# A conformer block on one core: the query projection in seven products instead of eight, placed at the turn of chunks

## The chip, the cores and the metric

The kernel runs on one core of one Trainium2 chip. The core has five engines that run beside each other: TensorE (PE in the profile) multiplies matrices into PSUM, VectorE (DVE) and ScalarE (ACT) do the elementwise work and empty PSUM, GpSimd (POOL) does small things, and SyncE (SP) issues the DMAs. The metric is the device time of one execution in microseconds (us), lower is better.

## The reference, cut to what matters

The reference is one conformer block on an input of 2 batches of 4000 tokens with 512 features: a feed-forward layer, self-attention with one head, a convolution module, a second feed-forward layer, each with a layer norm and a residual. What the change touches is the attention's query side:

```
h = _layernorm(x1)
q, k, v = h @ w_q, h @ w_k, h @ w_v
scores = einsum('btd,bsd->bts', q, k) * scale
attn = einsum('bts,bsd->btd', softmax(scores), v) @ w_o
x2 = x1 + attn
h = _layernorm(x2) @ w_pw1        # the first convolution product, 512 -> 1024
h = h[..., :512] * sigmoid(h[..., 512:])
```

## The kernel before, in words

**Tiling.** The tokens are cut into 16 chunks (`NCK`), 8 in each batch. A chunk has 512 tokens, the last of each batch 416, since 8 x 512 is more than 4000. The kernel has three stages: first feed-forward (to some 405 us), attention with the convolution beside it (to some 1380 us), and second feed-forward. The weights of queries and keys are folded into one matrix `M` beforehand, so that queries are `h M` and keys are `h` itself; likewise `w_v` and `w_o`.

**The attention loop.** `attention` (L2070) runs over the chunks `g` and, in each, over 32 steps `kt`, one for each tile of 128 keys. Two steps are called a pair, four make a quad. In chunk 0 each step makes a plain score product. From chunk 1 on steps 0, 1 and 30 are plain, step 31 holds the 32 keys that are left of the last tile, and steps 2 to 29 are seven *score quads* (`score_quad`, L2013). A quad multiplies 2x2 blocks with seven block products instead of eight (the Strassen-Winograd form): VectorE makes sums of the operands beforehand, TensorE computes products 5, 1, 6, 2, 7, 3, 4 in that order, and sums of products are joined on the way. A product here is four matmuls of 256 columns (208 in the chunks of 416 tokens). A quad has three PSUM banks, numbered 0, 1 and 2: `c`, `x` and `h`. Product 5 goes to `x` and ScalarE copies it to an SBUF tile m5; product 1 goes to `c`, and ScalarE copies that to `h`; product 6 is accumulated on `h`, and VectorE adds `h` and m5 into `x`; product 2 is accumulated on `c`; product 7 on `h`, and VectorE adds `h` and m5 once more; product 3 is accumulated on `x`, product 4 on `h`. So each product on `h` waits for an ACT or DVE instruction on it, and the next quad's banks are those of this one.

**The values** (`pv`, L1850) are in the same form: for each pair seven products of two matmuls, accumulated over the pairs in other banks. Products 2 and 4 of all pairs are put off to steps 2 to 6 of the next chunk (`late_third`, `units_late`, L2165). The exponentials of a pair therefore stay in a ring of `NR` places from when they are written to the next chunk's step 6 at most. At steps 0 and 1 the last sums of the chunk before are joined, and its row of softmax denominators (`lrow`) is written, stored to HBM and read back by query (`sum_row`, `sums_by_query`).

**The queries.** For a chunk `c`, `fetch_queries` (L1702) loads the tokens, transposed by DMA, to one of two slots of `lnT`; `q_group` (L1686) then makes 128 of the 512 query features with four matmuls of 512 columns, and ScalarE copies them out. Four groups make a chunk's queries: 16 matmuls of 512 columns (or 416) and four copies, at steps 16, 17 and 20 of the chunk before (for chunk 2 at steps 3 and 5). `q_sums` at steps 27 to 30 forms the sums of the queries that the score quads want.

**The convolution** of chunk `t` runs beside the attention of chunk `t + 2`: two *conv quads* at steps 2 to 7 on banks 7, 5, 3 and 4, and ScalarE's `taps_beside` at steps 8, 11, 14 and 17. Chunk 7 (416 tokens, its last tile shared with the other batch) is done plainly: `pair` (L2851) makes one of four feature blocks, two at steps 24 and 28 of chunk 8, two at steps 3 and 5 of chunk 9, and calls the taps of chunk 6 itself.

**What sets the order.** The program isn't emitted as written. `Plan` (L112) records every instruction, estimates its duration, and lists them anew engine by engine with a look-ahead of 16 us (8 us for TensorE), in six passes; each engine then runs its list strictly in order. `S.front(1000)` gives score quads a preference. All instructions are therefore recorded at one line, L95, and groups in the profile are told apart by tile names. In those names `s` are PSUM banks 0 to 3 and `y` banks 4 to 7. `work` holds `lnT`, `M`, the queries and the values' form 4; `xt` the sums for score quads and two of the value forms; `keys` keys and values; `sums` the exponentials; `wff` the convolution's work space. A row names what is written, then what is read: `s<-work` with 512 columns is a query group, `s<-xt` and `s<-work,keys` with 256 columns are score products, `y<-sums,keys` is a value product.

```
L2013  def score_quad(self, g, q, step):            # steps 0 to 3 = four kt
L2070  def attention(self, old, hook, between):
L2068      ASIDE = {3: (5, 7), 4: (5, 7), 5: (5, 7), 6: (5, 7), 16: (0,), 20: (0,)}   # banks lent to other products
L2753          S.planned(16000, 8000)
```

## Time and profile before

| | us |
|---|---|
| median of 3 runs (lowest to highest) | 1858.07 (1857.97 to 1860.41) |
| the profiled execution's own time | 1860.54 |
| its span, first to last instruction | 1855.0 |
| PE busy in the span | 1838.5 (99%) |
| DVE busy | 1439.8 (78%) |
| ACT busy | 1355.7 (73%) |
| POOL busy | 140.8 (8%) |
| mean granted TensorE clock | 0.999 of full speed |

The profiled execution took 1860.54 us, 2.47 us above the median of the three runs and close to the slowest of them; 5.54 us of it lie outside the span. PE's busy time counts matmuls that overlap in the pipeline, so it shows where PE had something under way, not that it did as much as it can. What one matmul costs is read from the timeline, from the start of one group to the start of the next.

### The profile page before, as it was taken

To read this page: it belongs to the slowest core of one execution; us is meant where nothing else is said; L and a number is where in the kernel's file an instruction comes from. 1 tells how busy PE (TensorE), PEld (TensorE's weight loads), DVE (VectorE), ACT (ScalarE), POOL (GpSimd) and SP (SyncE) were. 2 spreads that over 40 slices of the span, in tenths; PEclk is the share of its full clock that TensorE was granted. 3 is DMA by queue.
4 is the path that set the end of the run, shared out by engine and by line. 5 is a ranking of instruction groups with operands and counts; after the bars stand their busy time and mean duration, and the time that the engine had idled before them with its cause. 6 is when DMAs were issued, how large, how long until landed. Compare 5 with 4: busy or idle time off the path is not lost.

```text
span 1855.0 us, 40175 instructions
## 1 busy us (share of the span) xinstructions
PE 1838.5 (99%) x15922; PEld 1497.3 (81%) x15922; DVE 1439.8 (78%) x3108; ACT 1355.7 (73%) x2402; POOL 140.8 (8%) x356
## 2 busy tenths in 40 slices
PE   9999999999999999999999999999999999999998
PEld 6888888866878787888777788788875888888887
DVE  8889898868566777667875666766778988888896
ACT  6887777754656777677776876777768778778776
POOL 3000000000000000000000000000011000000000
PEclk9999999999999999999999999999999999999999
DMA  8333344288545655457954434543475222221211
GB/s 201 85 90 85 82 113 99 69 246 238 161 135 141 171 163 157 116 146 169 246 133 132 120 110 118 141 119 111 114 224 164 62 69 72 66 58 48 57 39 57
DMA packets 312521, 228.50 MB, mean 123 GB/s; under 512 B 191154, under 2 KB 283125, under 8 KB 312068
## 3 DMA queue, kind: packets, MB, share of 16 engines
q1 hardware_dynamic: 311796, 225.59, 45.2%
q8 instruction: 127, 2.08, 0.5%
q14 instruction: 70, 0.57, 0.1%
q10 hardware_dynamic: 528, 0.26, 0.0%
HBM read 128.99 MB, written 55.82 MB: 100 GB/s over the span
## 4 chain that ended last, share of the span: by engine, by line
PE 96%; ACT 1%; DVE 1%; DMA 1%; SPq 1%; issue 0%; POOL 0%; DVEq 0%
PE y L95 50%; PE s L95 45%; DVE work L95 1%; SPq L95 1%; ACT work L95 1%; DMA wff<-in_w_ff_a_dram 0%; DMA xt<-v12d 0%; DVE wff L95 0%; DMA keys<-tailsd 0%; ACT keys L95 0%; ACT sums L95 0%; DVE xt L95 0%; DMA work<-lrowd 0%; ACT xt L95 0%; DVE s L95 0%
## 5 line engine op out<-in xcount | busy, mean ns | idle before, releaser
L95 ACT ACTIVATE sums<-s 128x512 bf16<-128x512 f32 (+4 forms) x498 | 291.0, 585 | 131.2 <-PE s L95 127.4
L95 DVE TENSOR_TENSOR sums<-sums 128x512 bf16<-128x512 bf16 (+3 forms) x528 | 202.0, 399 | 87.2 <-ACT sums L95 75.4
L95 ACT ACTIVATE keys<-s 128x512 bf16<-128x512 f32 (+3 forms) x275 | 156.9, 574 | 134.4 <-PE s L95 110.9
L95 PE MATMUL y<-work,keys 128*128 128x256 bf16 x1920 | 244.5, 273 | 0.0
L95 PE MATMUL s<-sums 128*128 128x256 bf16 (+1 forms) x1428 | 212.5, 272 | 0.3 <-DVE s L95 0.3
L95 ACT ACTIVATE work<-xt,work 128x512 bf16<-128x512 bf16 x268 | 205.2, 785 | 8.8 <-DVE work L95 5.6
L95 PE MATMUL y<-wff,keys 128*128 128x256 bf16 (+3 forms) x1592 | 209.3, 276 | 0.0
L95 PEld LDWEIGHTS y<-work,keys 128*128 128x128 bf16 x1920 | 187.6, 98 | 22.6 <-DVE work L95 0.2
L95 PE MATMUL s<-work,keys 128*128 128x256 bf16 (+5 forms) x1400 | 205.3, 284 | 0.1
L95 PE MATMUL y<-sums,keys 128*128 128x256 bf16 (+1 forms) x1440 | 204.1, 270 | 0.1
L95 PE MATMUL y<-work,wff 128*128 128x256 bf16 (+3 forms) x1308 | 195.2, 272 | 0.8 <-ACT keys L95 0.8
L95 DVE TENSOR_TENSOR keys<-keys 128x1024 bf16<-128x1024 bf16 (+2 forms) x262 | 170.4, 664 | 22.6 <-ACT keys L95 17.8
L95 PEld LDWEIGHTS y<-wff,keys 128*128 128x128 bf16 (+1 forms) x1592 | 151.2, 98 | 29.9 <-issue 3.3
L95 DVE BATCH_NORM_STATS2 work<-xt 128x6 f32<-128x512 bf16 x251 | 163.0, 681 | 2.5 <-DMA xt<-in_x_dram 1.8
L95 PEld LDWEIGHTS y<-sums,keys 128*128 128x128 bf16 x1440 | 138.0, 98 | 25.3 <-issue 3.3
L95 PEld LDWEIGHTS s<-sums 128*128 128x128 bf16 x1428 | 139.0, 98 | 22.7 <-DVE s L95 0.6
L95 POOL TENSOR_TENSOR work<-work 128x4 f32<-128x4 f32 (+3 forms) x107 | 91.6, 859 | 765.1 <-DVE work L95 752.6
L95 PE MATMUL y<-sums,xt 128*128 128x256 bf16 (+1 forms) x960 | 146.1, 270 | 0.8 <-DMA xt<-v12d 0.8
L95 DVE TENSOR_TENSOR s<-s,xt 128x512 f32<-128x512 f32 (+1 forms) x105 | 72.4, 690 | 95.2 <-PE s L95 65.3
L95 PEld LDWEIGHTS s<-work,keys 128*128 128x128 bf16 (+1 forms) x1400 | 112.9, 97 | 40.9 <-ACT sums L95 2.2
L95 PEld LDWEIGHTS y<-work,wff 128*128 128x128 bf16 x1308 | 126.2, 98 | 17.9 <-issue 1.5
L95 PE MATMUL s<-xt,keys 128*128 128x256 bf16 (+1 forms) x872 | 132.5, 270 | 1.9 <-DVE s L95 1.7
(155 smaller groups left out, 3286.3 us busy)
## 6 DMA issues: line engine op xcount, KB each, us to landing
xt<-kfd SPq DMA_DIRECT2D x98, 384.0 KB, 3.3
xt<-v12d SPq DMA_DIRECT2D x105, 256.0 KB, 3.1
xd<-xt SPq DMA_DIRECT2D x28, 512.0 KB, 3.1
xt<-xd SPq DMA_DIRECT2D x28, 512.0 KB, 4.8
out_dram<-xt SPq DMA_DIRECT2D x14, 512.0 KB, 2.9
xt<-in_x_dram SPq DMA_DIRECT2D x13, 512.0 KB, 4.3
dcvd<-wff SPq DMA_DIRECT2D x48, 128.0 KB, 4.2
keys<-dcvd SPq DMA_DIRECT2D x12, 512.0 KB, 4.0
```

What stands on the lines that cost most here:

```text
L95: return getattr(eng, self.name)(*self.args, **self.kw)
```

## The change

The queries of chunks 2 to 15 are made by a new quad, `query_quad`, with 28 matmuls of 256 (or 208) columns in place of 16 of 512 (or 416). Chunks 0 and 1 keep `q_group`. The quad has the same banks 0, 1, 2 and the same order of products as a score quad. For chunk `g + 2` its first part (products 5 and 1) stands at step 31 of chunk `g`, the others (6 and 2; 7 and 3; 4) at steps 0 and 1 of chunk `g + 1`, around the plain scores of these steps; those now go to banks 0 and 1, before to 0 and 2. ScalarE makes five copies for it and VectorE two sums from PSUM.

It wants sums of the weights, made once (`query_weights`, four DVE instructions in steps 21 to 24 of chunk 0, the last one in place in `M`), and sums of the tokens (`query_sums`, four DVE instructions for each chunk, in steps 23 to 26 of the chunk two ahead of it). The tokens are thus fetched two chunks ahead, at step 9, into slot 1 of `lnT` (chunk 2's at step 21 of chunk 0, and into slot 1, before slot 0).

For room, the ring of exponentials has 18 places, before 20; the row of denominators moves to the convolution's work space, and the token sums stand there too. Since a place is now written again sooner, product 4 of the late values is dealt out differently over steps 3 to 6. The whole first convolution product of chunk 7 now stands in chunk 9, at steps 2 to 5, with three banks lent in turn, and the taps of chunk 6 at the steps of every other chunk.

```diff
-        self.NR, self.NTS = 20, 6
+        self.NR, self.NTS = 18, 6
...
+        oMF, o = o, o + 2 * row
...
-        lrow, self.b_lrow = C.view(oACC + 2048, CHUNK, F32, parts=1), C.buf("lrow", oACC + 2048, 4 * CHUNK)
-        self.lrow, self.lflat = lrow.rearrange("o (p t) -> o t p", t=TPC), lrow
...
+        homes = ((C, oACC + 2048), (C, oACC + 3072), (E, oMF))
+        self.MF = [R.view(o, D).rearrange("p (j f) -> p j f", j=2) for R, o in homes]
+        self.b_MF = [R.buf("MF", o, 2 * D) for R, o in homes]
...
+        lrow, self.b_lrow = W.view(12288, CHUNK, F32, parts=1), W.buf("lrow", 12288, 4 * CHUNK)
+        self.lrow, self.lflat = lrow.rearrange("o (p t) -> o t p", t=TPC), lrow
+        self.TF = [W.view(8192 + n * 1024, 2 * HC).rearrange("p (j k) -> p j k", j=2) for n in range(3)]
+        self.b_TF = [W.buf("TF", 8192 + n * 1024, 4 * HC) for n in range(3)]
...
-        return 1 if b or qc == 1 or qc > 2 else 0
+        return 1 if b or qc else 0
...
     def next_queries(self, g, kt, at):
-        if g + 1 < NCK and g != 1 and at <= kt < at + TPC:
-            self.fetch_queries((g + 1) // TCB, (g + 1) % TCB, kt - at)
-        if g == 0 and 24 <= kt < 24 + TPC:
-            self.fetch_queries(0, 2, kt - 24)
-        if self.any_score:
-            plan = {3: (0,), 4: (1,), 14: (2,), 16: (3,)} if g == 1 else {14: (0,), 16: (1,), 18: (2,), 20: (3,)}
-        else:
-            plan = {3: (0, 1), 5: (2, 3)} if g == 1 else {16: (0,), 17: (1, 2), 20: (3,)}
-        if g + 1 < NCK:
+        ahead = 1 if self.any_score or g == 0 else 2
+        if g + ahead < NCK and at <= kt < at + TPC:
+            self.fetch_queries((g + ahead) // TCB, (g + ahead) % TCB, kt - at)
+        if g == 0 and kt == 21 and not self.any_score:
+            self.fetch_queries(0, 2, 0)
+        if g + 1 < NCK and (g == 0 or self.any_score):
+            plan = {14: (0,), 16: (1,), 18: (2,), 20: (3,)} if self.any_score else {16: (0,), 17: (1, 2), 20: (3,)}
             for dc in plan.get(kt, ()):
                 self.q_group((g + 1) // TCB, (g + 1) % TCB, dc)
+
+    def query_weights(self, step):
+
+        a11, a12, a21, a22 = [self.M[:, 2 * k:2 * k + 2, f * HD:(f + 1) * HD] for f in range(2) for k in range(2)]
+        s1, s2, s4 = self.MF
+        b1, b2, b4 = [[b] for b in self.b_MF]
+        out, x, y, op, rd, wr = ((s1, a21, a22, ALU.add, [], b1), (s2, s1, a11, ALU.subtract, b1, b2),
+                                 (s4, a12, s2, ALU.subtract, b2, b4), (a21, a11, a21, ALU.subtract, [], [self.b_M]))[step]
+        self.S.op("DVE", lambda e: e.tensor_tensor(out=out, in0=x, in1=y, op=op), reads=rd + [self.b_M], writes=wr)
+
+    def query_sums(self, g, step):
+
+        b, qc = divmod(g, TCB)
+        sl, hw = self.query_slot(b, qc), width(g) // 2
+        lin = self.queries(qc, sl)[0]
+        at = lambda k, h: lin[:, 2 * k:2 * k + 2, h * hw:(h + 1) * hw]
+        t1, t2, t4 = [x[:, :, 0:hw] for x in self.TF]
+        b1, b2, b4 = [[x] for x in self.b_TF]
+        out, x, y, rd, wr = ((t1, at(0, 1), at(0, 0), [], b1), (t2, at(1, 1), t1, b1, b2), (t4, at(1, 0), t2, b2, b4),
+                             (at(0, 1), at(1, 1), at(0, 1), [], self.b_lnT[sl]))[step]
+        self.S.op("DVE", lambda e: e.tensor_tensor(out=out, in0=x, in1=y, op=ALU.subtract),
+                  reads=rd + self.b_lnT[sl], writes=wr)
+
+    def query_quad(self, g, step):
+
+        b, qc = divmod(g, TCB)
+        S, s, sl, W, hw = self.S, qc % 2, self.query_slot(b, qc), width(g), width(g) // 2
+        (c, b_c), (x, b_x), (h, b_h) = [self.bank(k) for k in range(3)]
+        m5, b_m5 = self.m5s[:, 0:W], self.b_m5s
+        lin = self.queries(qc, sl)[0]
+        two = lambda ap: ap.rearrange("p (u k) -> p u k", u=2)
+        part = lambda f, k: (lambda u, j: self.M[:, 2 * k + j, f * HD + u * 128:f * HD + (u + 1) * 128], self.b_M)
+        form = lambda m: (lambda u, j: self.MF[m][:, j, u * 128:(u + 1) * 128], self.b_MF[m])
+        at = lambda k, q: (lambda j: lin[:, 2 * k + j, q * hw:(q + 1) * hw], self.b_lnT[sl])
+        t_form = lambda m: (lambda j: self.TF[m][:, j, 0:hw], [self.b_TF[m]])
+        forms = {1: (part(0, 0), at(0, 0)), 2: (part(0, 1), at(1, 0)), 3: (form(2), at(1, 1)), 4: (part(1, 1), t_form(2)),
+                 5: (form(0), t_form(0)), 6: (form(1), t_form(1)), 7: (part(1, 0), at(0, 1))}
+        home = lambda f, q: (self.qT[s][:, 2 * f:2 * f + 2, q * hw:(q + 1) * hw], self.b_qT[s][2 * f:2 * f + 2])
+
+        def product(k, ps, b_ps, start=False):
+            (a, b_a), (m, b_m) = forms[k]
+            for u in range(2):
+                for j in range(2):
+                    self.mm(ps[:, u * hw:(u + 1) * hw], a(u, j), m(j), start and u == 0 and j == 0, u == 1 and j == 1,
+                            [b_a, *b_m], b_ps, skip_group_check=True)
+
+        def copy(src, b_src, f, q):
+            out, b_out = home(f, q)
+            self.act(out, two(src[:, 0:W]), AF.Copy, [b_src], b_out)
+
+        if step == 0:
+            product(5, x, b_x, True)
+            self.act(m5, x[:, 0:W], AF.Copy, [b_x], [b_m5])
+            product(1, c, b_c, True)
+            self.act(h[:, 0:W], c[:, 0:W], AF.Copy, [b_c], [b_h])
+        elif step == 1:
+            product(6, h, b_h)
+            S.op("DVE", lambda e: e.tensor_tensor(out=x[:, 0:W], in0=h[:, 0:W], in1=m5, op=ALU.add), reads=[b_h, b_m5], writes=[b_x])
+            product(2, c, b_c)
+            copy(c, b_c, 0, 0)
+        elif step == 2:
+            product(7, h, b_h)
+            out, b_out = home(1, 1)
+            S.op("DVE", lambda e: e.tensor_tensor(out=out, in0=two(h[:, 0:W]), in1=two(m5), op=ALU.add), reads=[b_h, b_m5], writes=b_out)
+            product(3, x, b_x)
+            copy(x, b_x, 0, 1)
+        else:
+            product(4, h, b_h)
+            copy(h, b_h, 1, 0)
     def p_home(self, g, i):
...
             product(4, h, b_h)
             exp(h[:, 0:W], b_h, 21)
-    ASIDE = {3: (5, 7), 4: (5, 7), 5: (5, 7), 6: (5, 7), 16: (0,), 20: (0,)}
+    ASIDE = {2: (5, 7, 3), 3: (3, 5, 7), 4: (7, 3, 5), 5: (5, 7, 3), 6: (3, 5, 7), 16: (0,), 20: (0,)}
     def attention(self, old, hook, between):
...
                     self.ring = [0, 1, 2]
                 else:
                     self.ring, self.rings["S"] = list(self.ASIDE.get(kt, (0, 1))), 0
+                if 0 < g < NCK - 1 and kt < 2:
+                    self.query_quad(g + 1, 1 if kt == 0 else 3)
                 if plain and kt < KT - 1 or kt < 2 or kt == KT - 2:
-                    ps, b_ps = self.scores(g, kt, None if plain else self.bank((0, 2)[kt] if kt < 2 else 0))
+                    ps, b_ps = self.scores(g, kt, None if plain else self.bank(kt if kt < 2 else 0))
                     if kt < KT - 2:
                         self.exp_pair(g, kt, ps, b_ps)
                     else:
...
                     S.front(1000)
                     self.score_quad(g, *divmod(kt - 2, 4))
                     S.front(0)
+                if g < NCK - 2:
+                    if kt == KT - 1:
+                        self.query_quad(g + 2, 0)
+                    if 23 <= kt < 27:
+                        self.query_sums(g + 2, kt - 23)
+                if 0 < g < NCK - 1 and kt == 0:
+                    self.query_quad(g + 1, 2)
+                if g == 0 and 21 <= kt < 25:
+                    self.query_weights(kt - 21)
                 if g == 0 and kt < 2:
                     self.pop(old // 2 if kt == 0 else old - old // 2)
                 if kt == (21 if g == 0 else 24 if g < NCK - 1 else 16):
...
         elif kt < 7:
             m = (kt - 2) * 6
             self.late_third(o, 2, range(m, min(m + 6, PAIRS)))
-            self.late_third(o, 4, range(max(m - PAIRS, 0), max(m + 6 - PAIRS, 0)))
+            self.late_third(o, 4, {3: range(1), 4: range(1, 3), 5: range(3, 9), 6: range(9, PAIRS)}.get(kt, ()))
         if kt == 9:
             self.ln_conv = self.nxt("ln", self.LN_SLOTS)
         for ti in {9: (0, 1), 13: (2, 3)}.get(kt, ()):
...
         def pair(t, jj, bank=None):
             self.conv_b(t, jj)
             self.after(1, lambda: self.conv_a(t, jj, bank))
-            if t:
+            if t and (any_score or t == tail):
                 self.after(3, lambda: self.taps_beside(t - 1, jj))
         def plain(t):
...
             if 0 <= g - 1 < tail and not plain(g - 1) and kt in TOKENS:
                 self.conv_sums(TOKENS.index(kt))
             t = g - 2
-            if 0 <= t < tail and not plain(t):
-                for n, step in CONV.get(kt, ()):
+            if 0 <= t < tail:
+                for n, step in CONV.get(kt, ()) if not plain(t) else ():
                     self.conv_quad(t, n, step)
                 if t and kt in TAPS:
                     self.taps_beside(t - 1, TAPS.index(kt))
         WEIGHTS, TOKENS, TAPS = (14, 16, 18, 20), (24, 25, 26, 27), (8, 11, 14, 17)
         CONV = {2: ((0, 0),), 3: ((0, 1),), 4: ((0, 2),), 5: ((0, 3), (1, 0)), 6: ((1, 1),), 7: ((1, 2), (1, 3))}
-        here, there = ((22, 27), (3, 8)) if any_score else ((24, 28), (3, 5))
+        here, there = ((22, 27), (3, 8)) if any_score else ((24, 28), (2, 3, 4, 5))
         def att_hook(g, kt):
             if g == 0 and kt == 8:
                 self.load(self.Wp1, i["w_pw1"].rearrange("(c p) f -> p c f", p=128), [self.b_Wp1])
-            if kt in here and (0 <= g - 1 < tail and plain(g - 1) or g - 1 == tail and here.index(kt) < self.KEEP):
+            if kt in here and (0 <= g - 1 < tail and any_score or g - 1 == tail and here.index(kt) < self.KEEP):
                 pair(g - 1, here.index(kt), self.bank(1) if kt == 24 else None)
             if 0 <= g - 2 < tail and kt in there and plain(g - 2):
-                pair(g - 2, 2 + there.index(kt))
+                pair(g - 2, there.index(kt) + 2 * any_score)
             if g == 0 and self.rest:
                 self.load_rest(FC + kt, 3)
             if kt == (12 if any_score else 22):
...
```

## The prediction

> **What bounds the kernel now.** I read the page first: engines' busy time and the chain that ended last.
>
> ```profile
> span 1855.0 us, 40175 instructions
> ...
> PE 1838.5 (99%) x15922; PEld 1497.3 (81%) x15922; DVE 1439.8 (78%) x3108; ACT 1355.7 (73%) x2402; POOL 140.8 (8%) x356
> ...
> PE 96%; ACT 1%; DVE 1%; DMA 1%; SPq 1%; issue 0%; POOL 0%; DVEq 0%
> ```
>
> TensorE is under way in 99% of the span and makes 96% of the chain. Since its busy time is modelled, I then asked for its waits in the attention alone, and for the busy times of that stretch and of one chunk.
>
> ```profile
> PE s L95 <- DVE s L95: 1.7, 2, 1.4
> PE y L95 <- DMA xt<-v12d: 0.8, 1, 0.8
> PE s L95 <- ACT sums L95: 0.7, 1, 0.7
> PE s L95 <- DVE work L95: 0.3, 1, 0.3
> PE s L95 <- ACT s L95: 0.3, 1, 0.3
> ```
>
> ```profile
> 405.00:1380.00 975.00, 970.75 (x8448) 775.02 (x8446) 671.82 (x1527) 693.03 (x1274) 56.39 (x241) 1.00 0.56 151
> 573.08:635.60 62.52, 62.52 (x544) 50.49 (x543) 42.49 (x98) 45.07 (x83) 3.56 (x16) 1.00 0.54 151
> ```
>
> The columns of the second fence are stretch, length, then PE, its weight loads, DVE, ACT and POOL, the granted clock and the DMA share. In 975 us TensorE waits 3.8 us (1.7 + 0.8 + 0.7 + 0.3 + 0.3); a full chunk of 62.5 us has none, at a full clock, and leaves DVE 20 us and ACT 17 us idle. The attention is bound by the sum of its matmuls, so a matmul taken away is time taken away, as long as what is put in its place doesn't make TensorE wait.
>
> **The change, part by part.** The first price is that of a matmul, from the start of a group to the start of the next.
>
> ```profile
> 607.34 1.89 PE L95 MATMUL s<-work 128*128 128x512 bf16 x8
> ...
> 609.06 0.38 PE L95 MATMUL y<-sums,xt 128*128 128x256 bf16 x2
> ...
> 802.17 1.57 PE L95 MATMUL s<-work 128*128 128x416 bf16 x8
> ...
> 803.58 0.38 PE L95 MATMUL y<-sums,xt 128*128 128x256 bf16 x2
> ...
> 855.48 0.87 PE L95 MATMUL s<-xt 128*128 128x208 bf16 x8
> ...
> 856.19 0.52 PE L95 MATMUL s<-work,keys 128*128 128x208 bf16 x4
> ```
>
> The two rows of `s<-work` are the query groups that go: 1.72 us for eight, 0.215 each, and 1.41 for eight narrow ones, 0.176. A product of 208 columns costs 0.71 / 8 = 0.089. For 256 columns, and for the handing to and fro on a bank, a score quad late in a chunk:
>
> ```profile
> 686.08 0.60 PE L95 MATMUL s<-work,keys 128*128 128x256 bf16 x4
> 686.52 0.82 PE L95 MATMUL y<-sums,xt 128*128 128x256 bf16 x6
> 686.78 0.58 ACT L95 ACTIVATE s<-s 128x512 f32<-128x512 f32 x1
> ...
> 687.17 0.38 PE L95 MATMUL y<-sums,keys 128*128 128x256 bf16 x2
> ...
> 687.42 0.61 PE L95 MATMUL s<-xt 128*128 128x256 bf16 x4
> ...
> 693.11 0.60 PE L95 MATMUL s<-xt 128*128 128x256 bf16 x4
> 693.55 0.60 PE L95 MATMUL s<-work,keys 128*128 128x256 bf16 x4
> 693.82 0.70 DVE L95 TENSOR_TENSOR s<-s,xt 128x512 f32<-128x512 f32 x1 [0.30 <-PE s L95]
> 693.99 0.38 PE L95 MATMUL y<-sums,keys 128*128 128x256 bf16 x2
> ...
> 694.20 0.60 PE L95 MATMUL s<-sums,keys 128*128 128x256 bf16 x4
> ...
> 694.64 0.60 PE L95 MATMUL s<-xt,keys 128*128 128x256 bf16 x4
> ...
> 695.08 0.60 PE L95 MATMUL s<-work,xt 128*128 128x256 bf16 x4
> ```
>
> From 693.11 to 695.08 lie 18 matmuls: 0.109 each. A chunk's queries cost 16 x 0.215 = 3.44 us now and 28 x 0.109 = 3.06 after, 0.38 less; in a narrow chunk 16 x 0.176 = 2.82 against 28 x 0.089 = 2.49, 0.33 less. Twelve full chunks and two narrow ones give 12 x 0.38 + 2 x 0.33 = **5.2 us less**. The written order of the changed kernel has just these counts: 192 wide and 32 narrow matmuls fewer, 336 and 56 half-width ones more.
>
> The same fence shows what a quad needs to run without a stop. Product 6 (693.11) is followed by DVE's sum (693.82 to 694.52) and product 7 (694.64); between the two products lie ten matmuls of other work, 1.09 us, and the sum is done 0.12 before product 7. Product 1 (686.08), ACT's copy to `h` (686.78 to 687.36), product 6 (687.42) make do with eight. In the changed kernel's order at a normal turn ten matmuls of 256 stand between products 1 and 6, ten between 6 and 7, and a plain score product with product 3 between 7 and 4 (0.86 + 0.44 = 1.30 us). So the new quad has the cover that score quads have. If the cover is gone, a busy DVE delays product 7 by at most one instruction of its own, 0.7 us, and the same for product 4; ACT delays product 6 by 0.6.
>
> Next, what the helpers get.
>
> ```profile
> L95 ACT ACTIVATE work<-s 128x512 bf16<-128x512 f32 x52 | 31.0, 596 | 10.6 <-PE s L95 10.0
> ...
> L95 PEld LDWEIGHTS s<-work 128*128 128x128 bf16 x482 | 46.5, 98 | 38.3 <-issue 0.4
> ...
> L95 DVE TENSOR_TENSOR xt<-work 128x512 bf16<-128x512 bf16 x26 | 10.9, 420 | 5.5 <-PE s L95 3.1 <-ACT work L95 2.4
> ...
> L95 DVE TENSOR_TENSOR work<-s,work 128x512 bf16<-128x512 f32 x14 | 9.5, 680 | 0.0
> ```
>
> DVE gets 4 x 0.42 + 2 x 0.68 = 3.0 us in each of 14 chunks and 1.7 us once for the weights, some 44 us, and is then busy in 716 of 975 us (73%). ACT gets one copy more in each, 14 x 0.6 = 8.4 us, and four move from steps 16 to 20 to the turn. On both I cost this at nothing, for the idle time above. PE's loads of weights grow by 12 a quad, 0.098 each, under matmuls of 0.109.
>
> The first turn, chunk 0 to 1, has less room:
>
> ```profile
> 445.00:455.00 10.00, 10.00 (x67) 6.27 (x66) 9.27 (x24) 4.18 (x7) 0.00 (x0) 1.00 0.53 172
> 455.00:465.00 10.00, 10.00 (x88) 7.85 (x86) 9.92 (x25) 3.46 (x6) 0.11 (x1) 1.00 0.69 210
> ```
>
> DVE is busy 19.2 of 20 us there, and the weights, the sums and two joins add 4.7. If nothing of it can slip, TensorE waits for the 3.9 us that don't fit; if DVE's other work slips into chunk 1, nothing (a full chunk has 20 us to spare). A gain is excluded, since work is only added. I take 0.2, near the lower end, because in the waits above TensorE waits hardly for DVE now, although DVE is as full.
>
> The rest has one answer each. Fetches: 14 moved by a chunk, the same count on SP; the sums that read them come 14 steps later.
>
> ```profile
> work<-keysd SPq DMA_TRANSPOSE x16, 5.0
> ```
>
> Landing takes 5.0 us and 14 of 32 steps are 27 us; only chunk 2's fetch, at step 21 of chunk 0, has its sums two steps (4 us) behind, and DVE would idle for the rest of a late landing. The order has other sums ahead of them, so nothing, at most 2 us once. Ring of 18: the exponentials of quad 0 overwrite pair 0 of the chunk before, and in the new order its late product 4 stands ahead of that quad's products 7 and 3; nothing. The row of denominators is rewritten to HBM by the same DMA and its new place is next wanted at step 5, four steps later; nothing. Chunk 7's convolution and the taps of chunk 6 keep their instructions and go from the fullest chunk to the emptier one:
>
> ```profile
> 878.55:945.00 66.45, 64.60 (x576) 50.84 (x574) 52.90 (x125) 49.47 (x92) 4.75 (x18) 1.00 0.95 228
> 945.00:1002.41 57.41, 57.41 (x502) 45.00 (x501) 37.53 (x84) 41.38 (x75) 3.72 (x14) 1.00 0.42 122
> ```
>
> ```profile
> 873.64 0.53 PE L95 MATMUL y<-sums,xt 128*128 128x208 bf16 x4 [0.85 <-DMA xt<-v12d]
> ...
> 917.09 0.61 PE L95 MATMUL s<-xt,keys 128*128 128x256 bf16 x4 [1.38 <-DVE s L95]
> ...
> 940.46 0.61 PE L95 MATMUL s<-xt,keys 128*128 128x256 bf16 x4 [0.33 <-DVE s L95]
> ```
>
> Waits of 0.85, 1.38 and 0.33 lie in and before chunk 8; they may vanish (2.6 us) or grow as much, for the order is planned anew from chunk 0 on. I take nothing.
>
> New waits in the quads: 105 score quads live with 3.8 us of waits, 0.036 each, so 14 more bring 0.5 (bounds: none, and the prices of the rivals below). Sum: -5.2 + 0.5 + 0.2 = -4.5 us. The profiled execution (1855.0 span and 5.54 around it, 1860.54) would take 1856.0; it stands 2.47 above the median, so that goes from 1858.07 to **1853.6**.
>
> **The rivals.** *Turns that wait a little* (same): the planner's order meets a DVE that is a fraction late at each turn. Any 0.8 to 5.2 us more of waits, 0.06 to 0.37 a turn, leaves 1854.4 to 1858.8 or so. For it: ten matmuls leave only 0.12 us to spare, and DVE gets two joins more at each turn. Against it: full chunks run without a wait.
>
> *The chain on bank `h`* (slower): three steps of a quad (copy, sum, sum) each come late by a third of an instruction because the turn's joins and the pair sums are ahead of them in DVE's order. It decides at (5.2 + 3.7) / 14 = 0.64 us a turn; at 0.7, one whole DVE instruction, it is 14 x 0.7 - 5.2 = 4.6 slower, 1862.7. Against it: the listed covers.
>
> *Half-width matmuls that cost more than half*: the change saves nothing once one costs 3.44 / 28 = 0.123 us; with the 12 extra weight loads laid bare, 12 x 0.098 x 14 = 16.5 us more, 1869.4. The rows speak against it: 18 in 1.97 us. The Trainium skill, TensorE: Matmul & The Clock Gate, section Back-to-back issue gap, has such a rule: in a stream of loads and matmuls 512 columns are said to take some 131 ns and 128 some 81, so 256 by a straight line some 98 as an estimate; queries would go from 2.1 to 2.7 us a chunk, and the kernel to some 9 us slower. This case's trace disagrees: 215 ns at 512 columns.
>
> *The waits around chunk 8 go too* (faster still): 5.2 + 2.6 = 7.8 less, 1850.3.
>
> **How the numbers follow.** A time within 0.2% (3.7 us) is about what a measurement can't tell from no change. My forecast (3.7 to 5.2 less, 1852.9 to 1854.3) has 0.56, the waits around chunk 8 gone 0.08: faster 0.64. Turns that wait a little 0.27: same. The chain on `h` 0.08 and dear half-width matmuls 0.01: slower 0.09. The range goes from 1850.3 (all waits gone) to 1858.2, where 5.3 us of new waits have eaten the gain.
>
> **What would show it.** Right: no query group of 512 columns after chunk 0, groups `s<-wff,work`, `s<-work` and `s<-work,sums` of four matmuls at the turns with 0.109 a matmul, a full chunk 0.4 us shorter between its step-30 scores, and TensorE's waits in the attention below 5 us. Wrong: waits of `PE s` for DVE or ACT at each turn, a wait for `DVE wff` (token sums late) or for the fetch, or the first turn longer by microseconds.

## The result, and the profile after

| | kernel before | changed kernel |
|---|---|---|
| median, us (lowest to highest), 20 runs each | 1858.99 (1857.91 to 1860.90) | 1855.68 (1854.00 to 1858.40) |
| the profiled execution: its time, its span | 1860.54, 1855.0 | 1857.54, 1853.4 |

The ratio is 0.9984 with a 95% interval of 0.9977 to 0.9991: 3.3 us less where 4.5 were forecast. The time lies in the range, but a gain of 0.16% is in the band that the forecast gave to "within 0.2%". The profiled execution of the changed kernel stands 1.9 us above its median, that of the kernel before 1.6. The changed kernel's executions spread: ten of the 20 have a span of 1850.0 to 1851.3 us, ten of 1852.0 to 1854.5, and its profile here (1853.4) and the two that follow (1855.9 and 1854.4) all come from long ones.

First the page of the changed kernel, then two stretches from its table of busy times (stretch, length, PE, its weight loads, DVE, ACT, POOL, granted clock, DMA share).

```profile
span 1853.4 us, 40681 instructions
...
PE 1832.9 (99%) x16090; PEld 1512.6 (82%) x16090; DVE 1475.7 (80%) x3196; ACT 1360.0 (73%) x2416; POOL 145.7 (8%) x356
...
PE 93%; DVE 3%; ACT 2%; DMA 1%; issue 0%; SPq 0%; POOL 0%; DVEq 0%; ACTq 0%
```

```profile
405.00:1380.00 975.00, 969.73 (x8635) 792.70 (x8634) 712.89 (x1625) 698.94 (x1291) 63.18 (x245) 1.00 0.56 152
572.30:633.90 61.60, 61.60 (x552) 51.40 (x551) 45.36 (x107) 45.26 (x84) 4.06 (x16) 1.00 0.53 146
```

DVE has 41 us more work in the attention (712.89 against 671.82), ACT 6 us more; a full chunk takes 61.6 us without an idle PE. In the chain of work that ended last, DVE's share went from 1% to 3%. Then the turn from chunk 4 to chunk 5, from the timeline of the changed kernel:

```profile
695.73 0.60 PE L95 MATMUL s<-wff,work 128*128 128x256 bf16 x4
...
696.17 0.60 PE L95 MATMUL s<-work 128*128 128x256 bf16 x4
...
696.61 0.60 PE L95 MATMUL y<-sums,keys 128*128 128x256 bf16 x4
...
697.04 0.60 PE L95 MATMUL s<-sums,keys 128*128 128x256 bf16 x4
...
697.70 0.60 PE L95 MATMUL s<-wff,work 128*128 128x256 bf16 x4
...
698.40 0.70 DVE L95 TENSOR_TENSOR s<-s,xt 128x512 f32<-128x512 f32 x1 [1.85 <-PE s L95]
698.57 0.82 PE L95 MATMUL y<-sums,xt 128*128 128x256 bf16 x6
...
699.23 0.60 PE L95 MATMUL s<-work 128*128 128x256 bf16 x4
```

These are products 5 and 1, ten other matmuls (eight of them shown), then product 6 (697.70), DVE's sum on it (done at 699.10) and product 7 (699.23). From 695.73 to 697.04 lie twelve matmuls, 0.109 each, and product 7 starts 0.13 after the sum: the new quad runs as the forecast had it. One of the 14 quads waits, at the turn from chunk 8 to 9, where product 6 stands 0.52 us for ACT's copy to `h`; the other 13 run without a stop:

```profile
939.12 0.61 PE L95 MATMUL s<-wff,work 128*128 128x256 bf16 x4 [0.52 <-ACT s L95]
```

Between the step-30 scores of two chunks that lie five full chunks apart, by ACT's rows (of before, then of after):

```profile
1002.41 0.60 ACT L95 ACTIVATE xt<-s 128x512 bf16<-128x512 f32 x1 [0.18 <-PE s L95]
...
1312.67 0.60 ACT L95 ACTIVATE xt<-s 128x512 bf16<-128x512 f32 x1 [0.31 <-PE s L95]
```

```profile
999.50 0.60 ACT L95 ACTIVATE xt<-s 128x512 bf16<-128x512 f32 x1 [0.70 <-PE s L95]
...
1307.66 0.59 ACT L95 ACTIVATE xt<-s 128x512 bf16<-128x512 f32 x1
```

310.26 us became 308.16, 0.42 less a chunk; 0.38 was forecast. This is one stretch of one pair of profiles: the same chunks take 308.57 and 309.42 us in the two later profiles of the changed kernel (after_again, after_pad88), 0.34 and 0.17 less a chunk. What stands against the gain are TensorE's waits: in the attention (405 to 1380 us), and in the second feed-forward, where the program is the same in both kernels. First the attention of the changed kernel, then the second feed-forward before and after (total, times, longest).

```profile
PE y L95 <- DVE wff L95: 1.2, 1, 1.2
PE s L95 <- ACT s L95: 0.8, 2, 0.5
PE s L95 <- DVE xt L95: 0.7, 1, 0.7
PE s L95 <- ACT sums L95: 0.7, 1, 0.7
PE s L95 <- DVE wff L95: 0.6, 1, 0.6
PE s L95 <- DVE sums L95: 0.5, 1, 0.5
PE s L95 <- DVE work L95: 0.3, 1, 0.3
```

```profile
PE s L95 <- ACT work L95: 1.0, 2, 0.8
PE y L95 <- ACT work L95: 0.8, 1, 0.8
PE y L95 <- ACT keys L95: 0.8, 1, 0.8
PE s L95 <- DVE work L95: 0.7, 2, 0.5
PE s L95 <- DVE s L95: 0.3, 1, 0.3
```

```profile
PE s L95 <- DVE sums L95: 1.4, 2, 0.7
...
PE y L95 <- DVE work L95: 0.6, 2, 0.3
```

The first are 4.8 us, before 3.8. The two rows of the last fence are new: 2.0 us in a stage that the change doesn't touch. Behind the largest wait of each stage lies a DMA. The largest wait of the attention, in chunk 8, and the first of the second feed-forward, from the timeline:

```profile
900.23 0.18 DVE L95 RECIPROCAL work<-work 128x4 f32<-128x4 f32 x1 [1.55 <-DMA work<-lrowd]
...
900.92 0.68 DVE L95 TENSOR_TENSOR wff<-y,wff 128x512 f32<-128x512 f32 x1
...
901.65 0.61 PE L95 MATMUL y<-work,wff 128*128 128x256 bf16 x4 [1.16 <-DVE wff L95]
```

```profile
1425.12 0.43 DVE L95 TENSOR_TENSOR sums<-work 128x512 bf16<-128x512 bf16 x1 [2.14 <-DMA work<-work]
...
1426.66 0.61 PE L95 MATMUL s<-sums,wff 128*128 128x256 bf16 x4 [0.70 <-DVE sums L95]
```

DVE stands 1.55 us at the row of denominators that is read back, the join behind it comes late, and TensorE waits 1.16 for it; likewise DVE stands 2.14 us at a transposed block and TensorE waits 0.70. In the attention DVE waits for DMAs more than twice as long as before: 10.7 us in the changed kernel (first fence), 4.4 before, of which the row of denominators is 3.9 (second fence).

```profile
DVE work L95 <- DMA work<-work: 4.8, 7, 1.0
DVE work L95 <- DMA work<-lrowd: 3.7, 4, 1.6
DVE wff L95 <- DMA dcvd<-wff: 2.2, 3, 1.3
```

```profile
DVE work L95 <- DMA work<-lrowd: 3.9, 5, 1.2
```

### The profile page after: what moved, and what is told of

It reads as the page before. It is cut to its first block, busy times and chain, and to the rows that moved or that the text cites. A ratio compares the mean times of both kernels' runs of the same rounds, so it can differ in the third digit from the quotient of the medians.

```text
span 1853.4 us, 40681 instructions
## 1 busy us (share of the span) xinstructions
PE 1832.9 (99%) x16090; PEld 1512.6 (82%) x16090; DVE 1475.7 (80%) x3196; ACT 1360.0 (73%) x2416; POOL 145.7 (8%) x356
## 4 chain that ended last, share of the span: by engine, by line
PE 93%; DVE 3%; ACT 2%; DMA 1%; issue 0%; SPq 0%; POOL 0%; DVEq 0%; ACTq 0%
PE y L95 49%; PE s L95 44%; DVE work L95 1%; ACT work L95 1%; DMA work<-work 1%; DVE wff L95 0%; DVE xt L95 0%; DVE sums L95 0%; DMA dcvd<-wff 0%; DVE s L95 0%; DVE keys L95 0%; ACT keys L95 0%; ACT sums L95 0%; DMA xt<-in_x_dram 0%; ACT s L95 0%
## 5 line engine op out<-in xcount | busy, mean ns | idle before, releaser
L95 PE MATMUL y<-sums,xt 128*128 128x256 bf16 (+1 forms) x960 | 141.1, 270 | 0.0
L95 DVE TENSOR_TENSOR s<-s,xt 128x512 f32<-128x512 f32 (+1 forms) x119 | 81.5, 685 | 66.1 <-PE s L95 56.7
```

What stands on the lines that cost most here:

```text
L95: return getattr(eng, self.name)(*self.args, **self.kw)
```

## The experiments

The first theory was this. The change saves its 5.2 us of matmuls; some come back as waits for late DMAs, and which DMA is late depends on where the fetches of TensorE's own instructions fall. In the views of DMA traffic there is a packet of 16 KB of instructions every 128 matmuls, and a transpose that was issued just before one landed late. From the changed kernel, DMA traffic from 1421 to 1425 us (the `q8` row is the fetch: packets, MB, share): the fetch takes 2.6% of 16 engines in 4 us, which is 1.7 us on one, and the transpose issued in that time took 4.1 us; over the whole stretch from 1380 to 1500 the median is 2.5.

```profile
q8 instruction: 1, 0.02, 2.6%
...
work<-work SPq DMA_TRANSPOSE x1, 4.1
```

168 more matmuls move the fetches against the work. The rivals: the place of the queries alone makes the gain; the turns wait; the rest of the edit (the ring, the row of denominators, the convolution's move) costs what is missing. Each group of runs had runs of the kernel before beside it on the same chip; times in us. "Outside" is a run's time less its span, medians both.

| kernel | what it is | time | span | outside | ratio to before, 95% |
|---|---|---|---|---|---|
| before, beside group 1 |  | 1859.39 | 1853.8 | 5.66 | |
| after_again (changed kernel) | no edit | 1856.47 | 1852.4 | 4.06 | 0.9982 (0.9973 to 0.9991) |
| before_pad40 | before, 40 matmuls more at its head | 1860.71 | 1855.4 | 5.66 | 1.0006 (0.9997 to 1.0015) |
| after_pad88 | changed, 88 matmuls more at its head | 1856.96 | 1853.2 | 3.92 | 0.9986 (0.9977 to 0.9995) |
| turn_groups | changed, query groups in place of quads | 1861.16 | 1856.2 | 5.22 | 1.0011 (1.0002 to 1.0020) |
| before, beside group 2 |  | 1859.23 | 1853.5 | 5.75 | |
| no_product4 | changed, quads without product 4 | 1850.35 | 1846.0 | 4.26 | 0.9953 (0.9938 to 0.9968) |
| before_filler | before, one-element instructions more on DVE and ACT | 1859.73 | 1853.9 | 5.79 | 1.0004 (0.9995 to 1.0013) |
| room_alone | before, with ring, deal and row's home | 1857.86 | 1853.7 | 4.04 | 0.9993 (0.9984 to 1.0002) |
| conv_alone | before, with the convolution's move | 1858.40 | 1853.1 | 5.14 | 0.9996 (0.9987 to 1.0005) |
| before, beside group 3 |  | 1859.54 | 1853.9 | 5.52 | |
| after_late | changed, planned with later transposes | 1857.52 | 1853.3 | 4.00 | 0.9994 (0.9985 to 1.0003) |
| after_late_all | changed, planned with later DMAs | 1854.18 | 1850.2 | 4.07 | 0.9973 (0.9963 to 0.9984) |
| before_late_all | before, planned with later DMAs | 1857.86 | 1853.7 | 4.06 | 0.9990 (0.9981 to 0.9999) |
| lrow_alone | before, with the row's home | 1857.91 | 1854.0 | 3.91 | 0.9992 (0.9983 to 1.0001) |

**The changed kernel again**, without an edit, on another chip.

> The changed kernel once more, nothing altered. Theory A (the quads save what was forecast, and part of it is lost again at the start of the second feed-forward, in some executions, because a fetch of TensorE's instructions falls into the flight of a token transpose there): times fall in two groups, about 4.7 us and about 1 us below the kernel before, and the trace reaches the end of the attention some 5 us earlier than the kernel before; it shows either two waits of about 1.4 us in all for transposes in the second feed-forward, with transposes that land after some 4.1 us, or none. Theory B (the rest of the forecast is lost in the attention, at the turns): one group near 3.3 us below, and the trace shows the loss before 1380 us.

2.9 us faster than before beside it, near the 3.3 of the first runs. But only 1.4 of it lie in the span (1853.8 to 1852.4); 1.6 lie outside, which no step of the prediction has. Its profile has the same waits: 2.0 us at chunk 8 and 1.9 new ones in the second feed-forward. Neither theory came out whole: the eleven times spread from 1854.74 to 1859.72 without two clear groups, the late transposes and their waits are there, but the last step-30 score comes only 1.1 us earlier than before (1367.75 against 1368.87), not 5. So there is loss in both stages.

**Moving the fetches alone.** 40 matmuls more before the first chunk in the kernel before, 88 more in the changed one, each in the time of the 13 wide warming matmuls that they replace; everything behind in the same order.

```diff
         for k in range(n):
             self.mm(ps[:, 0:CHUNK], self.zero[:, 0:128], self.zero, True, True, [self.b_zero], b_ps, inc=k == n - 1)
+        if self.S.plan:
+            small = lambda e: e.matmul(ps[:, 0:126], self.zero[:, 0:128], self.zero[:, 0:126], start=True, stop=True)
+            self.S.plan.pe[-1].emit[:] = [lambda k=k: self.S.emit_op("PE", small, [self.b_zero], [b_ps], k == 52) for k in range(53)]
```

These are the lines of before_pad40, 53 matmuls of 126 columns; after_pad88 has 101 of 66 in the same place.

> The kernel before, with the 13 warming matmuls of 512 columns at its head made 53 of 126 columns: the same columns, 40 matmuls more, so that every later block of TensorE's instructions is fetched where the changed kernel fetches it (168 matmuls more are 40 more than a block of 128). Theory A: 0.7 to 3 us slower than the kernel before, and the fourth transpose at the start of the second feed-forward lands after some 4.1 us, not 2.5. Theory C (the late transposes come from the change's moved buffers, or from chance): no difference, within 0.5 us, transposes at 2.5 us.

> The changed kernel with 101 warming matmuls of 66 columns for 13 of 512: 88 matmuls more, which with the change's 168 make two whole blocks of 128, so fetches fall in the second feed-forward where they fall in the kernel before. Theory A: 4.5 to 5 us faster than the kernel before, in one group of times, and no waits for transposes at the start of the second feed-forward. Theory C: as the changed kernel, 3.3 us faster, in two groups.

DVE's wait for transposes in the second feed-forward, in before_pad40 and then in after_pad88 (total, times, longest):

```profile
DVE sums L95 <- DMA work<-work: 2.3, 3, 1.9
```

```profile
DVE sums L95 <- DMA work<-work: 1.3, 3, 0.6
```

The waits move with the fetches: the kernel before, padded, gets a wait of 1.9 us where its longest was 0.6, and TensorE 0.8 us of waits with it; the changed kernel, padded, waits 1.3 us there in place of 4.6, and TensorE's 2.0 us are gone. The times follow in part: the first is 1.3 us slower, which lies in the 0.7 to 3 that were expected, but by its interval it can't be told from no change; the second, expected 4.5 to 5 us faster than before, is 2.4 faster and so no faster than the changed kernel. In its profile TensorE's waits in the attention have become 6.9 us. The place of the fetches decides where it waits; that it costs the changed kernel 2 us in all isn't shown by these two.

**The place alone.** The full-width query groups at the turn, two chunks ahead, on banks 1 and 2; no query quads and no sums for them.

```diff
-                    self.query_quad(g + 1, 1 if kt == 0 else 3)
+                    self.q_group((g + 1) // TCB, (g + 1) % TCB, 1 + 2 * kt, self.bank(2))
...
-                        self.query_quad(g + 2, 0)
-                    if 23 <= kt < 27:
-                        self.query_sums(g + 2, kt - 23)
+                        self.q_group((g + 2) // TCB, (g + 2) % TCB, 0, self.bank(1))
...
-                    self.query_quad(g + 1, 2)
-                if g == 0 and 21 <= kt < 25:
-                    self.query_weights(kt - 21)
+                    self.q_group((g + 1) // TCB, (g + 1) % TCB, 2, self.bank(1))
```

> The changed kernel with its placement alone: the queries of chunks 2 to 15 at the turn, two chunks ahead, but in four groups of four matmuls of full width, and without the sums of weights and tokens. Theory A (the gain is the columns saved): the attention takes as long as in the kernel before, within 1 us, 4.5 us more than in the changed one, and since the number of matmuls is that of the kernel before, the whole is within 1 us of it. Rival (the gain comes from moving the queries away from the steps in which ACT is fullest): at least 2 us faster than the kernel before.

1.8 us slower than before (2.4 in the span), 4.7 slower than the changed kernel (3.8 of it in the span). Theory A had it within 1 us of before, so the place gives nothing and costs a little; the gain is the columns that are no longer multiplied. In its profile DVE is as busy in the attention as before (672 us) and yet waits 5.5 us for DMAs, and TensorE waits 5.6: an order that is planned anew brings such waits without any new work for DVE.

**Product 4 left out.**

```diff
         else:
-            product(4, h, b_h)
             copy(h, b_h, 1, 0)
```

> The changed kernel without product 4 of the query quads: its output differs from the reference, since a quarter of the queries lacks a product. 48 matmuls of 256 columns and 8 of 208 are gone, 12 x 4 x 0.109 + 2 x 4 x 0.089 = 5.9 us. If the turns are bound by the sum of TensorE's matmuls, the time falls by 5 to 7 us against the changed kernel (1856.5 on the same chip: some 1850.5). If waits on bank h set the turns, the copy follows product 3 earlier but DVE's sums still come where they came: less than 3 us, 1853.5 or more.

Its span is 7.5 us below that of before beside it, against 1.4 for the changed kernel: 6.1 for matmuls worth 5.9 (four runs, on another chip than the runs of the changed kernel). What TensorE does at the turn is paid in full, as it is if the turns are bound by the sum of their matmuls. Product 4 is also a link in the chain on bank `h`, so this run alone doesn't rule that chain out; the changed kernel's profile does, where one quad of 14 waits. The rivals that see a chain on bank `h` or a wait at each turn fall.

**The rest of the edit in parts.** room_alone is the kernel before with the ring, the new deal of product 4 and the row's home; lrow_alone has the home only; conv_alone has the convolution's move.

```diff
-        self.NR, self.NTS = 20, 6
+        self.NR, self.NTS = 18, 6
...
-        lrow, self.b_lrow = C.view(oACC + 2048, CHUNK, F32, parts=1), C.buf("lrow", oACC + 2048, 4 * CHUNK)
...
+        lrow, self.b_lrow = W.view(12288, CHUNK, F32, parts=1), W.buf("lrow", 12288, 4 * CHUNK)
...
-            self.late_third(o, 4, range(max(m - PAIRS, 0), max(m + 6 - PAIRS, 0)))
+            self.late_third(o, 4, {3: range(1), 4: range(1, 3), 5: range(3, 9), 6: range(9, PAIRS)}.get(kt, ()))
```

> The kernel before with the ring of 18 places, the new deal of late product 4 and the row of denominators in its new home; no query quads, queries where they were. The prediction's theory: nothing, within 1 us of the kernel before (1859.4). The rival, that the smaller ring or the denser late products make TensorE wait and eat the gain that is missing: 2 us or more slower, 1861.4, with waits of y for DVE or of s for ACT early in the chunks.

> The kernel before with the narrow chunk's first convolution product and taps moved to chunk 8, and the tables of asides that go with them; queries as before. The prediction's theory: nothing on the whole, 1859.4 within 1 us, while single waits in and around chunk 8 (0.85, 1.38 and 0.33 in the kernel before) move. The rival, that the move costs what is missing: 2 us or more slower, with waits of over 2.5 us in all between the start of chunk 8 and its end. That the waits go altogether: 2.6 us faster, 1856.8.

In the span both are what the prediction said, nothing: 1853.7 and 1853.1 against 1853.5. Outside the span room_alone has 4.04 us in place of 5.75, as the changed kernel has, and by that it is 1.4 us faster than before, 0.4 past the 1 us that was expected.

**The time outside the span.** After the last instruction only fetches of 8 KB of instructions are left. From 2 us after the end of the span on there are two in the kernel before and one in the changed kernel (packets, MB, share):

```profile
q14 instruction: 2, 0.02, 0.9%
```

```profile
q14 instruction: 1, 0.01, 0.3%
```

The last one starts 5.2 us after the end of the span before, 3.3 after it in the changed kernel. Two tries at what decides it: the numbers of DVE's and ACT's instructions, and the home of the row.

```diff
+            left = {"DVE": 107, "ACT": 58}
...
+                if left[e] and seen[e] >= 900 and seen[e] % 6 == 0:
+                    left[e] -= 1
+                    if e == "DVE":
+                        S.emit_op(e, lambda v: v.memset(self.nrm[:, 0:1], 0.0), [], [self.b_nrm[0]], left[e] == 0)
+                    else:
+                        S.emit_op(e, lambda v: v.activation(self.nr1, self.eps2, AF.Copy), [self.b_eps2], [self.b_nr1], left[e] == 0)
```

These are the lines of before_filler; lrow_alone has the two `lrow` lines shown above.

> The kernel before with 107 one-element memsets on DVE and 58 one-element copies on ACT, spread over the attention and the stage after it, so that both engines have about as many instructions as in the changed kernel. In the runs so far the time outside the span is 4.1 us for the changed kernel (20 and 11 runs) and 5.7 for the kernel before (33 runs), and after the last instruction the trace of before shows one fetch of 8 KB of instructions more in a row. If those 1.6 us hang on how many instructions DVE and ACT have, the time outside falls to 4 to 4.5 here with the span unchanged within 1 us: 1857.8. If they hang on something else, 5.5 to 5.8 stays: 1859.4.

> The kernel before with the row of denominators in its new home and nothing else. With the ring of 18, the new deal and this home together the time outside the span was 4.04 us, as in the changed kernel, against 5.75 before, with the same span. If that comes with the home of the row, 4.0 to 4.4 outside and 1857.8 in all; if with the ring and the deal, 5.0 to 5.8 and 1859.3.

The numbers of instructions are not it: 5.79 stays. With the row's home it falls to 3.91; but before_late_all, below, leaves the row where it was and has 4.06, and turn_groups has the new home and 5.22. All kernels with 5.5 to 5.8 have the kernel before's order of instructions, and every one that was planned anew has less. Their profiles (before, before_pad40, before_filler) alone show a third such fetch in a row; the two kernels with 5.2 do not. What decides it stays open. The queries don't: it comes without them.

**A planner that reckons with late DMAs.** `Plan` reckons when a DMA lands; here it reckons 1.6 us later, for transposes in after_late, for every DMA in after_late_all and before_late_all.

```diff
-                n.land = pipe - s + 1000 + behind
+                n.land = pipe - s + (2600 if n.turn else 1000) + behind     # after_late
+                n.land = pipe - s + 2600 + behind                           # after_late_all, before_late_all
```

> The changed kernel with one figure of the planner changed: it reckons that a transposing DMA lands 1.6 us later, which is what a fetch of instructions beside it was seen to cost (4.1 to 4.7 us to landing in place of 2.5). Everything else as in the changed kernel. Theory (late transposes cost the stage after the attention its 2 to 3 us in the runs where a fetch meets them): the waits of TensorE for `DVE sums` after 1380 us go, the span's median falls from 1852 to about 1851 and its spread (1850 to 1855.9) closes from above; about 1855.0 in all. Rival (what is gained there is lost by the new order elsewhere, or the waits are not what the time hangs on): 1856 or more, as for the changed kernel.

> The same with 1.6 us for every DMA, not transposes alone. In the profiles of the changed kernel DVE waits 9 to 13 us for DMAs in the attention (`work<-work`, `work<-lrowd`, `dcvd<-wff`), 0.6 to 4.4 before, and TensorE 4.5 to 6.5 us there, 2 to 3.5 before. Theory (a fuller DVE hands its waits for DMAs on to TensorE): DVE's waits for DMAs fall below 5 us, TensorE's below 4, 1853.5 to 1854.5 in all. Rival (TensorE's waits are those of the quads' handing to and fro): TensorE's waits stay at 4.5 to 6.5, 1855.5 or more.

> The kernel before with 1.6 us more reckoned for every DMA: what that figure is worth without the change. If late DMAs only tell where DVE is full, nothing: 1859.3 within 1 us. If they cost the kernel before as much, 2 us or more less, 1857.3.

After_late_all, DVE's waits for DMAs in the attention and TensorE's waits there:

```profile
DVE work L95 <- DMA work<-work: 0.8, 1, 0.8
DVE work L95 <- DMA work<-lrowd: 0.3, 1, 0.3
```

```profile
PE s L95 <- ACT s L95: 1.5, 5, 0.4
PE s L95 <- DVE s L95: 0.7, 2, 0.5
PE s L95 <- ACT sums L95: 0.7, 1, 0.7
PE s L95 <- DVE sums L95: 0.6, 1, 0.6
PE s L95 <- ACT wff L95: 0.5, 1, 0.5
PE s L95 <- DVE work L95: 0.4, 1, 0.4
PE y L95 <- DVE xt L95: 0.2, 1, 0.2
```

With slack for every DMA the changed kernel takes 1854.18, 5.4 us less than before beside it, 3.7 of it in the span; the kernel before gains 0.2 in the span by the same figure (its time fell by 1.7, nearly all of it outside the span, and so between the two that were expected). Against after_again, on another chip, the span is 2.2 us shorter, and DVE's waits for DMAs in the attention fell from 10.7 us (after: 4.8 + 3.7 + 2.2) to 1.1. The new waits in the second feed-forward are gone too, though two transposes land as late there as in the changed kernel (4.0 and 4.1 us): DVE now has other work in its list ahead of them.

```profile
work<-work SPq DMA_TRANSPOSE x1, 4.0
```

```profile
1424.62 0.43 DVE L95 TENSOR_TENSOR sums<-work 128x512 bf16<-128x512 bf16 x1
```

So in the second feed-forward late transposes did cost the changed kernel some 2 us in the executions that were profiled. In the attention it isn't shown: DVE's waits are nearly gone there and TensorE's are not, and the new order itself may have done the rest. Of the kernels that make all products it is the fastest here and lies below both that were compared, though its interval meets that of after_again (0.9973 to 0.9991), and the two did not run beside each other.

Two expectations failed. TensorE's waits in the attention are 4.6 us, not below 4; what is left are hand-overs with ACT and DVE of 0.2 to 0.7 each, as the rival had it. And after_late, with slack for transposes alone, came to 1857.52 where 1855.0 was expected: it left DVE 0.5 us of its waits for transposes in the second feed-forward, but in its new order TensorE waits 6.5 us in the attention. Two orders of one program thus lie 3.1 us apart in the span (1853.3 and 1850.2).

## Why the prediction was right or wrong

- **5.2 us less of matmuls: right.** 0.109 a matmul at the turn, 0.42 a chunk between step-30 scores against 0.38 where TensorE hardly waits, and 6.1 us for the 5.9 of product 4 taken away. A half-width matmul costs 109 ns in the changed kernel where one of 512 columns cost 215, so the rival of dear half-width matmuls falls. The Trainium skill, TensorE: Matmul & The Clock Gate, section Back-to-back issue gap, gives some 131 ns for 512 columns in a stream of loads and matmuls; the 215 here don't agree with it.
- **Covers of the quad: right.** Product 7 starts 0.13 us after DVE's sum; 0.12 was reckoned. No chain on `h`: 13 of 14 quads run without a stop.
- **First turn +0.2; ring, row, deal, convolution 0:** nothing speaks against them. From the step-30 score of chunk 0 to that of chunk 1 the time went from 57.75 to 57.36 us, so the first turn cost nothing. Room and convolution alone leave the span unchanged within 0.4 us. That the waits around chunk 8 go too (1850.3) did not come: in chunk 8 and at its end they come to 2.7 and 3.0 us in the first two profiles of the changed kernel, at other places.
- **New waits in the quads 0.5: right in size, but in one quad.** The wait of 0.52 us at the turn from chunk 8 to 9 is all that the 14 quads have, in each of three profiles.
- **DVE's 44 us "at nothing, for the idle time", and no waits elsewhere: the step that failed.** The sum had a price for waits in the quads alone, and the new waits lie outside them. From the first step-30 score to the last TensorE waits 4.5, 5.1 and 6.5 us in three profiles of the changed order (after, after_again, after_pad88) against 3.5, 2.0 and 2.4 in three of the old (before, before_pad40, before_filler), some 2.7 more. The mean time between these two scores is 913.2 us against 914.1: 0.9 less, where 5.2 us of matmuls went, so 4.3 came back. The view counts a wait from the modelled end of the matmul before it, some 0.16 us after the next could have started (a row of four takes 0.60 us, and the next group starts after 0.44); with three waits more that is another 0.5. The last 1.1 us are in no wait that the view names, and stay open. All this is read from long executions: the three of the changed kernel lie 1.9, 3.3 and 1.6 us above their medians, those of the old order 1.6 above and 0.1 and 0.6 below. What a short one lacks isn't shown.
- **Why those waits came: in part argued.** The idle time was counted as a sum, but DVE's list runs in order, and one wait of 1.0 to 2.4 us for a DMA holds all joins behind it. In the attention DVE waits 10.7 to 12.5 us for DMAs in the three profiles of the changed order, 0.6 to 4.4 in those of the old. Some of that reaches TensorE, as the two cases shown above have it. Among these waits is one that the sum had not priced: the token sums share their space with the convolution's, and wait for its store (`DVE wff <- DMA dcvd<-wff`, 2.2 us); once DVE stands 1.26 us for it (to 1160.11) and TensorE then 0.68 (to 1162.22). The waits of `PE` for `DVE wff` that were named as a sign of late token sums do stand in the view (1.2 and 0.6 us), but none is before a quad. Whether a fuller DVE is the reason, or only the new order, isn't separated: turn_groups has such waits without a fuller DVE, and after_late_all has TensorE's waits nearly without DVE's.
- **The second feed-forward taken as unchanged: wrong.** Same instructions, other times of the instruction fetches: 2.0 and 1.9 us of new waits in both unpadded profiles, none with the fetches moved (after_pad88).
- **Why the time was close all the same: partly luck.** In the span the gain is about 1.4 us, not 4.5, in group 1; 1.6 more lie outside the span, where the sum had a constant. The two errors go against each other. "Turns that wait a little" named the right band of times (1854.4 to 1858.8) by a wrong mechanism: the turns don't wait but for one, other places do.

## What to carry to other kernels

Price work that goes to a helper by what its in-order queue waits for as well, not by its idle total alone: DVE, 73% busy in the attention, handed late DMAs on to TensorE. Where an order is planned ahead, try the landing times that DMAs have under disturbance; here 1.6 us more for every DMA went with a span 2.2 us shorter in the changed kernel and 0.2 in the kernel before, and for transposes alone with one 0.9 us longer. Expect an order that is planned anew to move the time by a few us on its own. And compare spans as well as times when a few us matter: half of the gain of group 1 came from outside the span, and without the queries.

## What the runs showed of the hardware that was not expected

TensorE's instructions come by DMA, 16 KB for some 128 matmuls with their weight loads (128 packets for 16090 matmuls), about every 14 us in the attention. The packet took 0.9 to 2.5 us on a DMA engine there, and small transfers beside it landed later: in six profiles (before, after, after_again, after_pad88, before_pad40, after_late_all) every transpose of the second feed-forward that was issued 0.3 to 2.1 us before such a packet landed after 3.0 to 4.5 us, those that met none after 2.4 to 3.2, mostly 2.5. The Trainium skill, Runtime: NRT & Kernel Launch, section Instruction fetch mechanics, has the same blocks of 16 KB and calls the cost of crossing one mostly hidden. The trace agrees as far as TensorE itself goes, which has no idle time in a chunk of 61.6 us with some four fetches; but other transfers can pay for it, and 40 or 88 matmuls in the head moved waits that came 1400 us later.

The time outside the span has levels (3.9 to 4.3, 5.1 to 5.2 and 5.5 to 5.8 us) as medians of a program's runs; what sets a program's level was not found.
